# Attention products of two heads, taken in step and in two held bursts

## Chip, core and metric

The kernel runs on one core of a Trainium2 chip. The metric is the device time of one execution in microseconds (us). Three runs of the kernel before gave 765.85, 768.72 and 768.73 us, median 768.72. The profile comes from one more execution.

## What is computed

Three layers follow each other, for 4 batches of 576 tokens and 512 channels (8 heads of 64). All inputs are float32 or wider and the result is float32.

```python
scores = scale * q @ k.T                       # per batch and head, 576 x 576
scores = where(causal, -1e9, scores + cum[:, None] - cum[None, :])   # cum = cumsum(log f)
attn   = exp(scores - max(scores))
attn   = attn / (sum(attn) + 1e-9)
x      = attn @ v                              # heads put side by side: 4 x 576 x 512
h      = relu(x @ w_in); u, v = halves of h
x      = (u * (w_spatial @ layernorm(v) + b)) @ w_out
k      = relu(mix_k(x) @ w_k)
out    = sigmoid(mix_r(x) @ w_r) * (k * k @ w_v)
```

## The kernel before, in words

**Pairs of heads.** The 32 heads of all batches go in 16 pairs. A pair's queries and keys are loaded, scaled, split in two float16 parts and transposed. `score` (L296) makes the scores, queries on partitions, in four steps `u` of up to 512 columns into PSUM tiles `s`; `rowmax` (L304, VectorE) takes the rows' maxima from them. `mrow` (L314) turns the maxima into a row by one matmul into a tile of the pool `psm`, and the row is written through DRAM into the operand `qA`. `scoreT` (L328) makes the scores a second time, keys on partitions, in four steps into tiles `t` (pool `pst`, two buffers), and ScalarE's exponential writes them to `e` (L339), one tile per head, four buffers. `causal` (L341, GpSimd) puts zeros above the diagonal of each of the five key chunks `c` of 128 tokens (the last has 64).

**Products and sums.** `pv` (L365) multiplies the chunks of `e` with the values: the stationary operand is 128x64, head 0 of the pair in columns 0 to 63 and so on partitions 0 to 63 of the output `o`, head 1 in columns 64 to 127. `o` is a tile of two PSUM banks in the pool `pso`, which has one buffer. Chunk 0 gives 512 and 64 columns, chunks 1 to 4 give 448, 320, 192 and 64. `sums` (L346) adds up the rows of `e` by a 128x32 block of ones, with four column blocks: two heads times the query ranges 0 to 383 and 384 to 575. Its output is a tile of `psm`, which holds 2 buffers and serves the MLP matmuls too. `e`, `v` and the ones are float32, and every such matmul stands as two records in the profile, so one pair has 24 records of `pv` and 32 of `sums`.

**After a pair.** ScalarE copies the sums (L358, L360) and the product (`head`, L383); the sums go through DRAM, are inverted, come back spread over the partitions as `sr` (`recip`), and GpSimd multiplies (`norm`, L400) and, with ScalarE, splits the result in the float16 tiles `xt` (`xhi`, `xlo`, L403 and L407).

**MLP and the end.** Of each batch, once its four pairs are there, `m1v`, `m1u` and `m2` (L516, L570, L587) run on TensorE between the attention of later pairs; the last batch's come after the attention. When the attention's pool is given back, its room is taken for the weights of the last layers, which are converted on ScalarE and VectorE; from about 457 us on TensorE works on those layers (L728).

**Order.** `plan_attention` (L623) and `plan_mlp` (L594) give every step a due time and a priority, `run` calls them in that order, and the framework's scheduler then puts the instructions of each engine in an order by priority and by when it takes them to be ready. The engines keep that order. Head `g` has its second scores at time `g`, so the two heads of a pair are one time unit apart; `sums` and `pv` come at `g + 1` and later, of priority 5. The scheduler may put any instruction that is ready between them.

Of the kernel before, what the change touches and what calls it, by code (L numbers as in the profile page):

```python
# [7 lines left out]
F32 = mybir.dt.float32  # L8
# [13 lines left out]
KB = [(128 * c, 128) for c in range(4)] + [(512, 64)]  # L22
# [6 lines left out]


P = dict(load=-8.0, sq=-5.6, ss=-5.2, sc=-5.0, hik=-4.6, lok=-4.25, hiq=-4.2, loq=-3.95, aux=-3.6,
         s=-2.4, m=-0.65, t=0.0, pv=1.0, out=1.35, rc=1.4, nr=1.9, xs=2.2, xl=2.4, mlp=2.7, mlplen=7.0, vload=-5.0, vsq=-3.0,
         w1=-3.8, w0=1.0, wsp=4.6)


def f32(ap):
# [3 lines left out]
class K:  # L40
# [273 lines left out]
    def mrow(self, p):  # L314

        nc = self.nc
        n, m = self.nm16[p % 2], self.nm[p % 2]
        nc.vector.tensor_copy(n[:, 0:10], m)
        nc.vector.tensor_tensor(n[:, 10:20], m, n[:, 0:10], ALU.subtract)
        ps = self.psm.tile([128, 512], F32, tag="m", name="mrow")  # L320
        nc.tensor.matmul(ps[:, 0:128], n, self.ident, start=True, stop=True)
        r = self.at.tile([20, 128], F16, tag="mr", bufs=2, name="mr")
        nc.vector.tensor_copy(r, ps[0:20, 0:128])
        d = self.hl.tile([2, 1280], F16, tag="md", bufs=2, name="md")
        nc.sync.dma_start(d.rearrange("i (c t) -> (i c) t", t=128), r)
        nc.sync.dma_start(self.T["qA", p % 3][67:69].rearrange("p c t -> p (c t)"), d)
# [14 lines left out]
    def causal(self, g, c):  # L341
        n = min(128, KB[c][1])
        e = self.e[g][:, EO[c]:EO[c] + n]
        self.nc.gpsimd.affine_select(out=e, in_=e, pattern=[[1, n]], compare_op=ALU.is_ge, fill=0.0, base=0, channel_multiplier=-1)  # L344

    def sums(self, p):  # L346

        o = self.psm.tile([128, 512], F32, tag="m", name="sums")
        last = {0: 2, 1: 4}
        for x, c in ((0, 0), (1, 0), (1, 1), (0, 1), (1, 2), (1, 3), (0, 2), (1, 4)):  # L350
            q0, q1 = ((0, 384), (384, 576))[x]
            f = max(q0, KB[c][0])
            off = EO[c] + f - KB[c][0]
            for h in range(2):
                r = 64 * h + 32 * x
                self.nc.tensor.matmul(o[r:r + 32, f - q0:q1 - q0], self.ones4 if c == 4 else self.ones[:, 0:32], self.e[2 * p + h][:, off:off + q1 - f], start=(c == 0), stop=(c == last[x]))  # L356
        t = self.at.tile([128, 384], F32, tag="sm", bufs=2, name="sm")
        self.nc.scalar.copy(t[:, 0:192], o[:, 0:192])  # L358
        for r in (slice(0, 32), slice(64, 96)):
            self.nc.scalar.copy(t[r, 192:384], o[r, 192:384])  # L360
        self.rd = [self.hl.tile([2, 576], F32, tag=f"rd{i}", bufs=2, name=f"rd{i}") for i in range(2)]
        self.nc.sync.dma_start(self.rd[0][:, 0:384], t[0:128:64])
        self.nc.sync.dma_start(self.rd[0][:, 384:576], t[32:128:64, 0:192])

    def pv(self, p, hf):  # L365

        b, pr = divmod(p, 4)
        if hf == 0:
            self.o[p] = self.pso.tile([128, 1024], F32, tag="o", name="o")
        o, v = self.o[p], self.v[b % 2]  # L370
        q0, q1 = ((0, 64), (64, 576))[hf]
        cs = [c for c in range(5) if KB[c][0] < q1]
        for c in cs:
            f = max(q0, KB[c][0])
            off = EO[c] + f - KB[c][0]
            for h in range(2):
                r = slice(64 * h, 64 * h + 64)
                self.nc.tensor.matmul(o[r, 448 + f:448 + q1], v[:, c, pr, r], self.e[2 * p + h][:, off:off + q1 - f], start=(c == 0), stop=(c == cs[-1]))  # L378

    def head(self, p):  # L380

# [232 lines left out]
    def add(self, t, prio, fn, *args):  # L614
        self.steps.append((t, prio, len(self.steps), fn, args))
# [7 lines left out]
    def plan_attention(self):  # L623
        add, G = self.add, self.B * self.H
        for p in range(G // 2):
            T = 2.0 * p
            if p > 1:
                add(T + P["load"], 9, self.load, p, "k")
                add(T + P["load"] + 0.3, 9, self.load, p, "q")
            for i, nm in enumerate("kq"):  # L630
                add(T + P["sq"] + 0.1 * i, 2, self.qksq, p, nm)
            add(T + P["ss"], 2, self.qkscale, p)
            add(T + P["hik"], 2, self.qkhi, p, "k", "act")
            add(T - 4.2, 2, self.crow, p)
            add(T + P["lok"], 2, self.qklo, p, "k")
            add(T + P["hiq"], 2, self.qkhi, p, "q", "dve")
            add(T + P["loq"], 2, self.qklo, p, "q")
            add(T + P["aux"], 2, self.kaux, p)
            add(T + P["aux"] + 0.1, 2, self.qaux, p)
            for h in range(2):  # L640
                for u in range(4):
                    add(T + P["s"] + h + 0.22 * u, 4, self.score, 2 * p + h, u)
                    add(T + P["s"] + h + 0.22 * u + 0.05, 1, self.rowmax, 2 * p + h, u)
            add(T + P["m"], 0, self.mrow, p)
        for g in range(G):
            for u in range(4):
                add(g + P["t"] + 0.22 * u, 0, self.scoreT, g, u)
            for c, u in ((0, 0), (1, 1), (2, 2), (3, 2), (4, 3)):
                add(g + P["t"] + 0.22 * u + 0.06, 1, self.causal, g, c)
            if g % 2:  # L650
                add(g + P["pv"], 5, self.sums, g // 2)
                for hf in range(2):
                    add(g + P["pv"] + 0.1 + 0.3 * hf, 5, self.pv, g // 2, hf)
                add(g + P["out"] + 0.1, 1, self.head, g // 2)
                add(g + P["rc"], 1, self.recip, g // 2)
                add(g + P["nr"], 2, self.norm, g // 2)
                add(g + P["xs"], 2, self.xhi, g // 2)
                add(g + P["xl"], 2, self.xlo, g // 2)
        for b in range(self.B):
            for c in range(5):  # L660
                add(8 * b + P["vload"] + 0.2 * c if b else -3.2, 9, self.vload, b, c)
                add(8 * b + P["vsq"] + 0.3 * c, 3, self.vsq, b, c)
            add(8 * b + P["vsq"] + 1.8, 3, self.vscale, b)
# [222 lines left out]
```

## Time and profile before

| | before |
|---|---|
| runs, median of 3 | 768.72 us |
| profiled execution, its own time | 764.88 us |
| its span, first to last instruction | 762.8 us |
| TensorE busy (matmuls) | 693.1 us, 91% |
| VectorE, ScalarE, GpSimd busy | 416.2, 377.1, 158.3 us |
| mean granted TensorE clock | 0.977 |

Busy time is the union of an engine's instructions in the span. In the timeline a matmul lasts until its last value is out, which overlaps the next matmul; in the chain of waits a piece counts only the time that it adds to the chain. PEclk is the granted TensorE clock as a share of 2.4 GHz.

### The profile page before, as it was taken

The page shows a single profiled execution, that of the slowest core. Times are in us where ns is not written, and L with a number is a line of the kernel's source. Part 1 is how long each engine was busy: PE and PEld are TensorE (multiplying, and loading weights), DVE is VectorE, ACT ScalarE, POOL GpSimd, SP SyncE. Part 2 cuts the span into 40 slices and gives each one's busy share as a digit, 9 for nine tenths or more (in the row PEclk, how much of TensorE's full clock was granted, in tenths as well). Part 3 has the DMA queues.
Part 4 walks back from the last instruction along what each step waited for, and adds up shares of the span by engine and source line. Part 5 has one row for each costly group of instructions (what it writes and reads, how often), then busy time and mean ns, then how long its engine had stood idle before and what let it go on. Part 6 is the DMA issues. An engine that isn't in the chain of part 4 may idle for free.

```text
span 762.8 us, 11881 instructions
## 1 busy us (share of the span) xinstructions
PE 693.1 (91%) x4166; PEld 469.0 (61%) x4166; DVE 416.2 (55%) x1147; ACT 377.1 (49%) x772; POOL 158.3 (21%) x369
## 2 busy tenths in 40 slices
PE   0378969999999999999998679999999999999997
PEld 0233433455665556655665448788888888888896
DVE  4886656477545556546014878987415522542342
ACT  4626666676535754346413737757325423622431
POOL 6022523555313533335012200000000000000000
PEclk9998979999999999999999889999999999999999
DMA  9985597476366333320014455460101100010010
GB/s 220 200 195 116 111 181 130 103 158 144 90 168 145 65 70 68 98 54 17 17 50 141 160 160 161 135 188 6 56 1 41 56 1 14 1 56 0 1 56 27
DMA packets 130747, 69.82 MB, mean 92 GB/s; under 512 B 114736, under 2 KB 115408, under 8 KB 130688
## 3 DMA queue, kind: packets, MB, share of 16 engines
q1 hardware_dynamic: 128096, 67.89, 36.9%
q10 hardware_dynamic: 2592, 1.19, 0.6%
q8 instruction: 32, 0.52, 0.3%
q14 instruction: 27, 0.22, 0.1%
HBM read 42.06 MB, written 9.79 MB: 68 GB/s over the span
## 4 chain that ended last, share of the span: by engine, by line
PE 69%; DMA 12%; DVE 7%; SPq 3%; ACT 3%; issue 2%; POOL 2%; DVEq 0%; ACTq 0%; POOLq 0%
PE m L728 38%; PE o L378 6%; PE sums L356 4%; PE s L302 4%; PE t L335 4%; PE m1u L570 4%; PE m L587 4%; PE m1v L516 3%; DMA wst<-in_moe_w_in_dram 2%; DMA wst<-in_moe_w_k_dram 2%; DMA v<-in_v_dram 1%; DMA qA<-qT 1%; DVE junk L311 1%; DMA wb<-in_moe_b_spatial_dram 1%; DMA rd<-r 1%
## 5 line engine op out<-in xcount | busy, mean ns | idle before, releaser
L311 DVE CUSTOM_DVE_ANT_0 junk<-s,mask 128x512 bf16<-128x512 f32 (+4 forms) x160 | 76.1, 476 | 68.4 <-PE s L302 61.9
L728 PE MATMUL m<-xx,moe_w_k 128*128 128x512 f32 (+1 forms) x480 | 106.0, 369 | 0.4 <-ACT x L723 0.4
L728 PE MATMUL m<-moe_w_v,k 128*128 128x512 f32 x432 | 104.2, 390 | 0.0
L339 ACT ACTIVATE e<-t,qa 128x512 f32<-128x512 f32 (+1 forms) x128 | 73.9, 591 | 53.9 <-PE t L335 52.1
L728 PEld LDWEIGHTS m<-xx,moe_w_k 128*128 128x128 f32 x480 | 83.9, 188 | 16.9 <-ACT x L723 0.9
L728 PEld LDWEIGHTS m<-moe_w_v,k 128*128 128x128 f32 x432 | 80.7, 188 | 17.0
L344 POOL TENSOR_SCALAR_AFFINE_SELECT e<-e 128x128 f32<-128x128 f32 (+1 forms) x160 | 54.5, 355 | 155.3 <-ACT e L339 153.4
L378 PE MATMUL o<-e,v 128*64 128x64 f32 (+4 forms) x384 | 76.8, 408 | 1.4 <-POOL e L344 1.3
L302 PE MATMUL s<-kT,qT 128*128 128x512 f16 (+2 forms) x192 | 56.0, 305 | 19.6 <-DVE nm L311 11.8
L764 DVE TENSOR_TENSOR tmp<-tmp 128x512 f32<-128x512 f32 (+1 forms) x40 | 25.5, 638 | 86.7 <-ACT tmp L763 86.7
L728 PE MATMUL m<-gh,moe_w_out 128*128 128x512 f32 (+1 forms) x240 | 55.3, 381 | 3.5 <-DVE u L590 3.4
L763 ACT ACTIVATE tmp<-m 128x512 f32<-128x512 f32 (+1 forms) x40 | 22.1, 556 | 70.2 <-PE m L728 70.2
L570 PE MATMUL m1u<-xt,win 128*128 128x288 f16 x384 | 53.0, 291 | 3.9 <-ACT u L572 3.9
L516 PE MATMUL m1v<-win,xt 128*128 128x512 f16 x240 | 56.5, 379 | 0.0
L302 PE MATMUL s<-kA,qA 67*128 67x512 f16 (+2 forms) x192 | 51.0, 304 | 5.8 <-DMA kA<-kT 3.9
L587 PE MATMUL m<-wspT,vn 128*128 128x288 f16 x384 | 53.9, 291 | 1.3 <-DVE u L590 1.3
L335 PE MATMUL t<-qA,kA 69*128 69x512 f16 (+2 forms) x192 | 51.0, 291 | 1.7 <-ACT e L339 1.7
L728 PEld LDWEIGHTS m<-gh,moe_w_out 128*128 128x128 f32 x240 | 43.3, 193 | 13.3 <-DVE u L590 3.7
L728 PE MATMUL m<-moe_w_r,xx 128*128 128x512 f32 x216 | 51.2, 394 | 0.0
L335 PE MATMUL t<-qT,kT 128*128 128x512 f16 (+2 forms) x192 | 51.1, 290 | 0.0
L570 PEld LDWEIGHTS <-win 128*128 128x128 f16 x384 | 36.6, 99 | 18.5 <-issue 7.8
L728 PEld LDWEIGHTS m<-moe_w_r,xx 128*128 128x128 f32 x216 | 40.4, 187 | 9.9
(164 smaller groups left out, 1061.2 us busy)
## 6 DMA issues: line engine op xcount, KB each, us to landing
sr<-rd SPq DMA_DIRECT2D x32, 144.0 KB
gd<-u SPq DMA_DIRECT2D x16, 288.0 KB
out_dram<-o SPq DMA_DIRECT2D x18, 256.0 KB
knat<-in_k_dram SPq DMA_DIRECT2D x32, 128.0 KB
v<-in_v_dram SPq DMA_DIRECT2D x32, 128.0 KB
g<-gd SPq DMA_DIRECT2D x16, 256.0 KB
wst<-in_moe_w_k_dram SPq DMA_DIRECT2D x8, 512.0 KB
wst<-in_moe_w_v_dram SPq DMA_DIRECT2D x8, 512.0 KB
```

Of the source, the lines that this page charges most:

```text
L302: self.nc.tensor.matmul(s[:, o:o + n], self.tok(qn, p, h, 128 * ib - 64, 128)[0:r], self.tok(kn, p, h, k0, n)[0:r], start=(j == 0), stop=( ...
L311: self.nc.vector.tensor_tensor_reduce(out=self.junk[r0:, 0:n], in0=self.s[u % 2][r0:, o:o + n], in1=self.mask[r0:, m0:m0 + n], op0=ALU.add ...
L335: self.nc.tensor.matmul(t[:, o:o + n], self.tok(kn, p, h, 128 * c, 128)[0:r], self.tok(qn, p, h, q0, n)[0:r], start=(j == 0), stop=(j == 1))
L339: self.nc.scalar.activation(self.e[g][:, 512 * u:512 * u + n], t[:, 0:n], AF.Exp, scale=self.qa[p][:, 5:6])
L344: self.nc.gpsimd.affine_select(out=e, in_=e, pattern=[[1, n]], compare_op=ALU.is_ge, fill=0.0, base=0, channel_multiplier=-1)
L356: self.nc.tensor.matmul(o[r:r + 32, f - q0:q1 - q0], self.ones4 if c == 4 else self.ones[:, 0:32], self.e[2 * p + h][:, off:off + q1 - f], ...
L378: self.nc.tensor.matmul(o[r, 448 + f:448 + q1], v[:, c, pr, r], self.e[2 * p + h][:, off:off + q1 - f], start=(c == 0), stop=(c == cs[-1]))
L516: nc.tensor.matmul(self.m1p, xt[:, xs, 128 * j:128 * j + 128], self.win[:, ws, kc, 512:1024], start=(kc == 0 and n == 0), stop=(kc == 3 an ...
L570: self.nc.tensor.matmul(o, self.win[:, ws, kc, fs], self.xt[(4 * b + kc) % 8][:, xs, ts_], start=(kc == 0 and n == 0), stop=(kc == 3 and n ...
L587: nc.tensor.matmul(o, pairs[n][0], pairs[n][1], start=(n == 0), stop=(n == 13))
L728: self.nc.tensor.matmul(out, l, r, start=(first and j == 0), stop=(last and j == len(pairs) - 1))
L764: nc.vector.tensor_tensor(tmp[:, 0:n], tmp[:, 0:n], tmp[:, 0:n], ALU.mult)
```

## The change

The two heads of a pair go in step: `scoreT` and `causal` of step `u` come for the even head at `0.44 u` and for the odd head 0.22 later, from the same start. `products` replaces the calls of `sums` and `pv`. Part 0 is the product of chunks 0 and 1; part 1 is the sums and then the product of chunks 2, 3 and 4. Within a part every matmul depends on the one before it by `chain` (an order on TensorE, no wait), and all are traced at a priority raised by 300. The sums go into columns 0 to 383 of `o` itself instead of a tile of `psm`; their chunks come in another order; and the tile of `mrow` is one of the score tiles `s` (pool `pss`, two buffers). The arithmetic is the same.

```diff
+         ... t=0.0, tu=0.44, th=0.22, pv0=0.2, pv1=0.9, out=1.35, ...
+PRIO = 300
@@ mrow
-        ps = self.psm.tile([128, 512], F32, tag="m", name="mrow")
+        ps = self.pss.tile([128, 512], F32, tag="s", name="mrow")
@@ new
+    def chain(self, ins):
+        if self.last is not None:
+            self.tc.add_manual_dep(ins.ins, self.last.ins.name, mybir.DependencyInfo(mybir.DependencyClass.NoSync, mybir.DependencyReason.DATA))
+        self.last = ins
+
+    def products(self, p, part):
+        self.last = None
+        with self.tc.high_priority(PRIO):
+            if part == 0:
+                self.o[p] = self.pso.tile([128, 1024], F32, tag="o", name="o")
+                self.pv(p, ((0, 64, 576), (1, 64, 576), (0, 0, 64)))
+            else:
+                self.sums(p)
+                self.pv(p, ((2, 64, 576), (3, 64, 576), (4, 64, 576)))
@@ sums
-        o = self.psm.tile([128, 512], F32, tag="m", name="sums")
-        for x, c in ((0, 0), (1, 0), (1, 1), (0, 1), (1, 2), (1, 3), (0, 2), (1, 4)):
+        o = self.o[p]
+        ends = ((0, 2), (3, 0))
+        for x, c in ((1, 3), (0, 0), (1, 4), (1, 2), (0, 1), (1, 1), (0, 2), (1, 0)):
...
-            for h in range(2):
+            for h in (1, 0):
...
-                self.nc.tensor.matmul(..., start=(c == 0), stop=(c == last[x]))
+                self.chain(self.nc.tensor.matmul(..., start=(c == ends[x][0]), stop=(c == ends[x][1])))
@@ pv
-        q0, q1 = ((0, 64), (64, 576))[hf]
-        cs = [c for c in range(5) if KB[c][0] < q1]
-        for c in cs:
+        for c, q0, q1 in pieces:
...
-            for h in range(2):
+            for h in (1, 0):
@@ plan_attention
+            h = g % 2
-                add(g + P["t"] + 0.22 * u, 0, self.scoreT, g, u)
+                add(g - h + P["t"] + P["tu"] * u + P["th"] * h, 0, self.scoreT, g, u)
...
-                add(g + P["pv"], 5, self.sums, g // 2)
-                for hf in range(2):
-                    add(g + P["pv"] + 0.1 + 0.3 * hf, 5, self.pv, g // 2, hf)
+                add(g + P["pv0"], 5, self.products, g // 2, 0)
+                add(g + P["pv1"], 5, self.products, g // 2, 1)
```

**First place: TensorE, the first pair's products and sums.** Before, `e_403` is head 0 and `e_485` head 1; L378 are products, L356 sums.

```order
L356 MATMUL sums_580<-e_485,ones_121 32x192
L356 MATMUL sums_580<-e_403,ones_121 32x256
L378 MATMUL o_618<-e_485,v0_142 64x512
L378 MATMUL o_618<-e_403,v0_142 64x448
L356 MATMUL sums_580<-e_485,ones_121 32x256
L356 MATMUL sums_580<-e_403,ones_121 32x192
L378 MATMUL o_618<-e_485,v0_142 64x448
L378 MATMUL o_618<-e_403,v0_142 64x320
L356 MATMUL sums_580<-e_485,ones_121 32x192
L356 MATMUL sums_580<-e_403,ones_121 32x192
```

Head 0 is one chunk ahead of head 1 in the products, so that 512 columns of one stand beside 448 of the other, and sums stand between. After the change (`e_423` is head 1, `e_403` head 0; L376 are sums, L394 products):

```order
L376 MATMUL o_516<-e_423,ones_121 32x192
L376 MATMUL o_516<-e_403,ones_121 32x192
L376 MATMUL o_516<-e_423,ones_121 32x128
L376 MATMUL o_516<-e_403,ones_121 32x128
L376 MATMUL o_516<-e_423,ones_121 32x192
L376 MATMUL o_516<-e_403,ones_121 32x192
L394 MATMUL o_516<-e_423,v0_142 64x320
L394 MATMUL o_516<-e_403,v0_142 64x320
L394 MATMUL o_516<-e_423,v0_142 64x192
L394 MATMUL o_516<-e_403,v0_142 64x192
L394 MATMUL o_516<-e_423,v0_142 64x64
L394 MATMUL o_516<-e_403,v0_142 64x64
```

Equal chunks of the two heads stand side by side, and sums and products are apart. Over the whole program the 192 products stand in 89 uninterrupted stretches before and in 39 after, the 256 sums in 44 and in 32: the sums of every pair are in two pieces, of 4 and of 12 matmuls, with other work between.

**Second place: TensorE, the last pair's sums.** The rows `m_` are the MLP's L587 (L603 after the change), 14 matmuls to a number; the third batch has 8 such numbers. Before:

```order
L587 MATMUL m_4398<-wspT,v_105 128x288
L378 MATMUL o<-e,v_143 64x448
L378 MATMUL o<-e,v_143 64x320 x2
L356 MATMUL sums<-e,ones 32x384 x2
L356 MATMUL sums<-e,ones 32x192 x4
L356 MATMUL sums<-e,ones 32x256 x2
L356 MATMUL sums<-e,ones 32x192 x4
L356 MATMUL sums<-e,ones 32x128 x2
L356 MATMUL sums<-e,ones_123 32x64 x2
L587 LDWEIGHTS vn
L587 MATMUL m_4442<-wspT,vn 128x288
```

After:

```order
L603 MATMUL m_4535<-wspT,v_105 128x288
L376 MATMUL o<-e,ones_123 32x64 x2
L376 MATMUL o<-e,ones 32x192 x2
L376 MATMUL o<-e,ones 32x256 x2
L376 MATMUL o<-e,ones 32x192 x2
L376 MATMUL o<-e,ones 32x128 x2
L376 MATMUL o<-e,ones 32x192 x2
L603 LDWEIGHTS v_105
L603 MATMUL m_4535<-wspT,v_105 128x288
L603 LDWEIGHTS vn
L603 MATMUL m_4552<-wspT,vn 128x288
```

`m_4398` is the first of the third batch's eight numbers, `m_4535` the sixth. Behind the last sums stand 210 matmuls of `m2`, 48 of `m1v` and 96 of `m1u` before, and 141, 44 and 96 after: 69 of `m2` and 4 of `m1v` have moved ahead of them.

## Rows read from the trace of the kernel before

**Rows 1.** Windows: busy time of each engine by stage, granted clock, DMA share.

```profile
core 0: us, PE busy (x) PEld busy (x) DVE busy (x) ACT busy (x) POOL busy (x), PEclk, DMA share, GB/s
40.00:117.00 77.00, 62.89 (x372) 28.38 (x371) 49.94 (x193) 44.05 (x99) 23.84 (x50) 0.89 0.75 152
117.00:392.00 275.00, 270.88 (x2056) 153.76 (x2056) 145.53 (x523) 149.83 (x331) 108.11 (x243) 0.99 0.42 90
```

**Rows 2.** Waits of TensorE from 117 to 392 us: total, times, longest.

```profile
PE o L378 <- POOL e L344: 1.3, 1, 1.3
```

**Rows 3.** The same windows, products (L378) alone.

```profile
40.00:117.00 77.00, 14.83 (x74) 5.00 (x74) 0.89 0.75 152
117.00:392.00 275.00, 61.99 (x312) 22.80 (x311) 0.99 0.42 90
```

**Rows 4.** The same windows, sums (L356) alone.

```profile
40.00:117.00 77.00, 13.22 (x96) 4.45 (x96) 0.89 0.75 152
117.00:392.00 275.00, 29.78 (x416) 16.05 (x416) 0.99 0.42 90
```

**Rows 5.** Chain of waits, first pair, broken up (start, us, what).

```profile
59.34 0.76 PE sums L356 x3
61.34 0.77 PE sums L356 x8
65.00 0.68 PE o L378 x3
66.13 0.47 PE o L378 x3
```

**Rows 6.** Chain of waits, one pair from 319 us on.

```profile
319.70 1.00 PE o L378 x3
320.87 0.90 PE o L378 x3
324.03 1.55 PE sums L356 x24
325.74 1.01 PE o L378 x6
327.74 0.26 PE o L378 x2
```

**Rows 7.** Timeline of TensorE: products without a break, and a pair's first 20 ns.

```profile
95.19 2.69 PE L378 MATMUL o<-e,v 128*64 128x512 f32 x16
...
207.28 0.64 PE L378 MATMUL o<-e,v 128*64 128x512 f32 x2
```

**Rows 8.** Chain of waits, around the last pair's sums and behind them.

```profile
335.31 2.59 PE m1v L516 x12
...
387.87 1.55 PE sums L356 x24
389.42 1.83 PE m L587 x14
400.38 1.42 POOL xo L400
457.54 10.21 PE m L728 x36
```

**Rows 9.** Chain of waits, early.

```profile
95.53 2.23 DMA rd<-r
99.67 7.51 DMA wb<-in_moe_b_spatial_dram
```

**Rows 10.** Groups of instructions: busy, mean ns of one, idle before.

```profile
L339 ACT ACTIVATE e<-t,qa 128x512 f32<-128x512 f32 (+1 forms) x128 | 73.9, 591 | 53.9 <-PE t L335 52.1 <-PE s L302 1.2
L344 POOL TENSOR_SCALAR_AFFINE_SELECT e<-e 128x128 f32<-128x128 f32 (+1 forms) x160 | 54.5, 355 | 155.3 <-ACT e L339 153.4 <-DVE nq L270 0.8
L383 ACT COPY xo<-o 128x576 f32<-128x576 f32 x16 | 10.2, 638 | 15.2 <-PE o L378 15.1
L360 ACT COPY sm<-sums 32x192 f32<-32x192 f32 x32 | 9.8, 307 | 0.2
```

More of the change, by code (lines that the diff above doesn't have):

```diff
@@ L31 @@
 P = dict(load=-8.0, sq=-5.6, ss=-5.2, sc=-5.0, hik=-4.6, lok=-4.25, hiq=-4.2, loq=-3.95, aux=-3.6,
-         s=-2.4, m=-0.65, t=0.0, pv=1.0, out=1.35, rc=1.4, nr=1.9, xs=2.2, xl=2.4, mlp=2.7, mlplen=7.0, vload=-5.0, vsq=-3.0,
+         s=-2.4, m=-0.65, t=0.0, tu=0.44, th=0.22, pv0=0.2, pv1=0.9, out=1.35, rc=1.4, nr=1.9, xs=2.2, xl=2.4, mlp=2.7, mlplen=7.0, vload=-5.0, vsq=-3.0,
          w1=-3.8, w0=1.0, wsp=4.6)
+PRIO = 300
 def f32(ap):
@@ L344, in causal @@
         self.nc.gpsimd.affine_select(out=e, in_=e, pattern=[[1, n]], compare_op=ALU.is_ge, fill=0.0, base=0, channel_multiplier=-1)
+    def chain(self, ins):
[11 more added lines that the diff above has]
+                self.pv(p, ((2, 64, 576), (3, 64, 576), (4, 64, 576)))
     def sums(self, p):
-        o = self.psm.tile([128, 512], F32, tag="m", name="sums")
-        last = {0: 2, 1: 4}
-        for x, c in ((0, 0), (1, 0), (1, 1), (0, 1), (1, 2), (1, 3), (0, 2), (1, 4)):
+        o = self.o[p]
+        ends = ((0, 2), (3, 0))
+        for x, c in ((1, 3), (0, 0), (1, 4), (1, 2), (0, 1), (1, 1), (0, 2), (1, 0)):
             q0, q1 = ((0, 384), (384, 576))[x]
@@ L353, in sums @@
             off = EO[c] + f - KB[c][0]
-            for h in range(2):
+            for h in (1, 0):
                 r = 64 * h + 32 * x
-                self.nc.tensor.matmul(o[r:r + 32, f - q0:q1 - q0], self.ones4 if c == 4 else self.ones[:, 0:32], self.e[2 * p + h][:, off:off + q1 - f], start=(c == 0), stop=(c == last[x]))
+                self.chain(self.nc.tensor.matmul(o[r:r + 32, f - q0:q1 - q0], self.ones4 if c == 4 else self.ones[:, 0:32], self.e[2 * p + h][:, off:off + q1 - f], start=(c == ends[x][0]), stop=(c == ends[x][1])))
         t = self.at.tile([128, 384], F32, tag="sm", bufs=2, name="sm")
@@ L363, in sums, with pv @@
         self.nc.sync.dma_start(self.rd[0][:, 384:576], t[32:128:64, 0:192])
-    def pv(self, p, hf):
+    def pv(self, p, pieces):
         b, pr = divmod(p, 4)
-        if hf == 0:
-            self.o[p] = self.pso.tile([128, 1024], F32, tag="o", name="o")
         o, v = self.o[p], self.v[b % 2]
-        q0, q1 = ((0, 64), (64, 576))[hf]
-        cs = [c for c in range(5) if KB[c][0] < q1]
-        for c in cs:
+        for c, q0, q1 in pieces:
             f = max(q0, KB[c][0])
             off = EO[c] + f - KB[c][0]
-            for h in range(2):
+            for h in (1, 0):
                 r = slice(64 * h, 64 * h + 64)
-                self.nc.tensor.matmul(o[r, 448 + f:448 + q1], v[:, c, pr, r], self.e[2 * p + h][:, off:off + q1 - f], start=(c == 0), stop=(c == cs[-1]))
+                self.chain(self.nc.tensor.matmul(o[r, 448 + f:448 + q1], v[:, c, pr, r], self.e[2 * p + h][:, off:off + q1 - f], start=(c == 0), stop=(c == 4 or q1 == 64)))
     def head(self, p):
@@ L645, in plan_attention @@
         for g in range(G):
+            h = g % 2
             for u in range(4):
-                add(g + P["t"] + 0.22 * u, 0, self.scoreT, g, u)
+                add(g - h + P["t"] + P["tu"] * u + P["th"] * h, 0, self.scoreT, g, u)
             for c, u in ((0, 0), (1, 1), (2, 2), (3, 2), (4, 3)):
-                add(g + P["t"] + 0.22 * u + 0.06, 1, self.causal, g, c)
+                add(g - h + P["t"] + P["tu"] * u + P["th"] * h + 0.06, 1, self.causal, g, c)
             if g % 2:
-                add(g + P["pv"], 5, self.sums, g // 2)
-                for hf in range(2):
-                    add(g + P["pv"] + 0.1 + 0.3 * hf, 5, self.pv, g // 2, hf)
+                add(g + P["pv0"], 5, self.products, g // 2, 0)
+                add(g + P["pv1"], 5, self.products, g // 2, 1)
                 add(g + P["out"] + 0.1, 1, self.head, g // 2)
```

## The prediction, before the changed kernel had run

> **What bounds the kernel now.** I read the windows by stage first, then the same windows for the two lines that the change moves, then the waits of TensorE, then single stretches of the chain and the timeline. In the windows [rows 1] the reader sees two stages. From 117 to 392 us TensorE is busy 270.88 of 275 us, VectorE 145.53, ScalarE 149.83, GpSimd 108.11, and the DMA engines 42%: TensorE alone bounds it, and a microsecond less of its work is a microsecond. From 40 to 117 us TensorE is busy 62.89 of 77 us at a granted clock of 0.89 of 2.4 GHz, so a part of that stage ran at 1.2 GHz, and transfers take their turn in the chain. In that first bound stage TensorE hardly waits: the longest wait of a product was one of 1.3 us, for the mask [rows 2].
>
> The products take 61.99 us of the bound stage [rows 3] and the sums 29.78 us [rows 4]. These are 312 of 384 and 416 of 512 records, so 13 of the 16 pairs (24 and 32 records each), at 4.77 and 2.29 us a pair.
>
> Next I looked at what a product costs where. Two matmuls of the two heads run beside each other: a stretch of 16 records takes 2.69 us, and two records, of 512 and 448 columns, had both begun within 20 ns [rows 7]. In such a pair the longer one sets the time. Broken up, a fragment costs 1.00 us when its longer member has 512 columns, 0.90 with 448 [rows 6], 0.68 with 320, 0.47 with 192 [rows 5] and 0.26 with 64 [rows 6]. The order of the kernel before puts head 0 a chunk ahead of head 1. The ladder of one pair is then 64 alone, 64 beside 512, 512 beside 448, 448 beside 320, then 320, 192 and 64 in one stretch, and 64 alone: 0.26 + 1.00 + 1.00 + 0.90 + 1.01 + 0.26 = 4.43 us, near the 4.77 busy, in which the tails overlap other work.
>
> **The change, part by part.** *Products in step.* Equal chunks stand side by side, so each length is paid once. Part 0 is 512, 448 and 64: 1.00 + 0.90 + 0.26 = 2.16. Part 1 is 320, 192 and 64: 0.68 + 0.47 + 0.26 = 1.41. Joined stretches are cheaper: the 16 records of rows 7, whose longer members are 512, 448, 320 and 192, would be 3.05 us in fragments and took 2.69, so each of the three seams costs 0.12. With four seams less the two parts are 1.92 + 1.17 = 3.09 us. The gain is 4.43 - 3.09 = 1.34 a pair, 17 us for 13 pairs. In 7 pairs other work still divides a part, 0.12 each, so I take 16. If no seam were saved it would be 4.43 - 3.57 = 0.86 a pair, 11 us; that is the other end.
>
> The trace speaks for this term, a rule speaks against it. The Trainium skill, page "TensorE: Matmul & The Clock Gate", Part 3, says that a weight load overlaps running matmuls only where their row groups differ; both heads here use all 128 rows and differ in columns only. By that rule the heads would run one after the other, holding them together would win nothing, and the sum would lose its 16 us. The trace disagrees: the two records that began within 20 ns have the same rows [rows 7].
>
> *Sums.* Where they stand in one stretch, all four column blocks run together in 1.55 us [rows 6]. After the change each pair's sums are in two pieces. The first, 192 and 384 columns for both heads, costs what such a group cost before, 0.76 [rows 5]. The second has 64 + 3 x 192 in its longer block: 1.55 less one piece of 192, which is half of the 0.77 for two [rows 5], 1.17. Together 1.93, and with a tail for each, which busy time counts, 2.07 against 2.29 now. The tail is an estimate, 0.07, from the ladder's 4.77 busy against 4.43 over about five stretches. That is 0.2 a pair, 3 us for the 13; between 1 and 5, because early pairs were in many pieces and late ones in one.
>
> *Early pairs.* The three pairs before 117 us take 14.83 + 13.22 = 28 us [rows 3, 4] and would take 3 x 5.0 = 15, so at most 13 us are there. But TensorE is idle 14 of these 77 us, and the chain passes the DMA of the MLP's bias, 7.51 us [rows 9], whose issue stands on SP's queue behind the first pairs' sums and their way through DRAM. I take 4 us, between 0 and 10.
>
> *MLP work moved ahead.* Behind the last pair's sums comes a chain that TensorE doesn't set: copies, DRAM, `norm` at 400.38 and the weights of the last layers, with L728 from 457.54 on [rows 8]. So the end of those sums at 389.42 is what has to come earlier. In the new order 69 matmuls of `m2` and 4 of `m1v` more stand ahead of it, at 1.83 / 14 = 0.13 and 2.59 / 12 = 0.22 us [rows 8]: 9.9 us, taken as 10. Before, they filled the 11 us between the sums and `norm`, where TensorE had nothing else to do, so that moving them saves nothing behind; it gives back over half of the gain.
>
> *New waits.* The held parts wait for both heads' exponentials and masks, 0.59 and 0.36 us each [rows 10]. In the order some ten matmuls of other work usually stand between the last second score that a part needs and the part, and TensorE waits so little now [rows 2] that I take 2 us in all; the ends are 0 and the 30 us of the rival below. `mrow`'s tile takes one of two score buffers for one matmul and one short copy; it gives the MLP's pool both of its buffers back. I count the two as nothing; the work that hides them is the MLP between 117 and 392 us. Without that cover, before 117 us, a score step waits for that copy, some 0.3 us a pair, one us for three pairs, inside the range.
>
> *SP and GpSimd.* No DMA is added or taken away. The masks keep their number; each pair's ten come in a shorter time, on an engine that is busy 108 of 275 us [rows 1].
>
> **The sum**: -16 - 3 - 4 + 10 + 2 = -11 us. The profiled execution's own time is 764.88 us, which gives 754; the median of the three runs is 768.72, 3.8 above it, so for a median I forecast 757 us, 1.5% less. A difference of 0.5%, 3.8 us, is about what a measurement of this kernel tells from none.
>
> **Rivals.** *The gain is absorbed.* TensorE saves 19 us of work between 117 and 392 us, and 10 go for the moved MLP. If the early stage gives nothing and the remaining 9 are lost to waits of 0.6 us a pair, on scores, transfers or copies that TensorE now reaches sooner, the time stays near 768. For it: the chain of the early stage passes transfers [rows 9]. Against it: no other engine is busy over 55% of the bound stage [rows 1]. Chance 0.20.
>
> *The held parts stall.* TensorE keeps its order, and everything behind a part waits with it, the other head's scores too. If at each of the two parts of 16 pairs it waits for one exponential and one mask, 0.95 us [rows 10], 30 us are added: 787 us. It turns the result to slower from a mean wait of 15 / 32 = 0.47 us a part on. For it: both heads' steps come to ScalarE at once now, with two `t` buffers for both. Against it: the one wait of this kind in the bound stage [rows 2]. Chance 0.08.
>
> *The one buffer of `o`.* The sums lie in `o` now, so the next pair's part 0 waits not only for `head` but for the sums' copies: 0.64 + 2 x 0.31 = 1.25 us on ScalarE [rows 10]. With nothing between the pairs that is 20 us, 777 in all; it decides from three quarters of it on. In the order long stretches of scores and MLP stand between, but for one place (fourth and fifth pair) with six matmuls. The Trainium skill, page "PSUM — Partial Sum Buffer", section "PSUM bank collisions raise a hardware error", says why such a wait can't be left out: two engines must not touch one bank and quadrant at once. No row here shows such a collision. Chance 0.04.
>
> *Heads don't run together*, by the rule above: the 16 us of the products stay away, 757 + 16 = 773. Against it stand the ladder's present times. Chance 0.02.
>
> **How the numbers follow.** Forecast 0.66, all of it faster. No change: 0.20. Slower: 0.08 + 0.04 + 0.02 = 0.14. The range goes down to 744: 6 us if the early pairs give 10, 2 without new waits, 2 from the sums' upper end, and 3 if the stage behind the attention gets shorter by a part of the moved MLP. It goes up to 770, which takes in the first rival. What lies outside is the slower cases and a little below, under 2 in 10.
>
> **What the changed profile would show.** Right: products at about 3.3 us busy a pair and sums at 2.1, together 86 instead of 119.8 us; the last pair's sums end about 11 us earlier, near 378 us; L728 begins as much earlier, and the time from there to the end is the same. Wrong: waits of products or sums for `e` of more than 10 us in all; idle time before part 0 that ends with ScalarE's copy of `o`; products still over 4 us a pair; or the sums' end earlier while L728 begins when it did.

## The result and the profile after

The changed kernel took 746.66 us (median of 4 runs, 744.77 to 748.49) against 768.51 us (4 runs of before beside it). The ratio is 0.972, 95% interval 0.969 to 0.976: 2.8% faster, where 1.5% was forecast. The profiled execution took 748.21 us, 16.7 less than that of before, with a span of 746.5.

The windows by stage, all engines (columns as in [rows 1]):

```profile
40.00:117.00 77.00, 60.13 (x408) 29.79 (x409) 57.49 (x217) 48.55 (x111) 28.34 (x59) 0.84 0.75 166
117.00:392.00 275.00, 264.03 (x2143) 155.74 (x2139) 144.86 (x508) 144.57 (x318) 98.93 (x236) 0.99 0.41 92
```

Products (L394) alone, which answer to [rows 3]:

```profile
40.00:117.00 77.00, 14.82 (x84) 5.95 (x84) 0.84 0.75 166
117.00:392.00 275.00, 39.81 (x300) 19.09 (x300) 0.99 0.41 92
```

Sums (L376) alone, which answer to [rows 4]:

```profile
40.00:117.00 77.00, 6.75 (x96) 2.86 (x96) 0.84 0.75 166
117.00:392.00 275.00, 28.81 (x416) 12.60 (x416) 0.99 0.41 92
```

In the later stage a pair's 24 product records took 39.81 x 24 / 300 = 3.18 us busy, where it was 4.77. The sums lost only 1 us there and halved in the early stage. TensorE is less full now: 264 of 275 us.

Waits of TensorE from 117 to 392 us (total, times, longest), the longest totals, which answer to [rows 2]:

```profile
PE o L376 <- POOL e L347: 3.2, 4, 1.3
PE s L305 <- DMA kA<-kT: 1.9, 1, 1.9
PE mrow L324 <- DVE nmh L322: 1.9, 2, 1.3
PE o L394 <- POOL e L347: 1.2, 1, 1.2
```

The held parts do wait for masks now, sums above all, a little at a time.

Chain of waits (start, us, what): a pair's parts, and the last sums to the last layers, which answer to [rows 6, 8]:

```profile
142.10 1.13 PE o L394 x12
152.24 1.88 PE o L394 x12
...
216.11 1.01 PE o L394 x4
217.66 1.02 PE o L394 x8
221.24 0.81 PE o L376 x6
226.40 1.21 PE o L376 x18
...
379.52 1.24 PE o L376 x18
...
391.57 1.41 POOL xo L416
...
466.04 3.98 PE m L744 x16
```

A held part 0 costs 1.88 us, divided in two 2.03; part 1 costs 1.13; the two pieces of sums 0.8 and 1.2. The last sums end at 380.76 us instead of 389.42.

To see where the 16 us arose I cut the span at the last sums' end. Windows of the kernel before, same columns:

```profile
40.00:120.00 80.00, 65.17 (x385) 29.46 (x384) 52.37 (x209) 46.91 (x107) 25.29 (x55) 0.89 0.75 152
120.00:389.40 269.40, 266.00 (x2019) 150.83 (x2019) 142.80 (x507) 146.02 (x319) 106.66 (x239) 0.99 0.43 91
389.40:762.80 373.40, 353.73 (x1732) 283.69 (x1730) 193.22 (x357) 162.84 (x301) 11.55 (x31) 0.98 0.21 67
```

and of the changed kernel:

```profile
40.00:120.00 80.00, 62.62 (x426) 30.71 (x427) 60.46 (x227) 51.55 (x118) 30.89 (x65) 0.85 0.73 162
120.00:380.70 260.70, 250.24 (x2045) 147.69 (x2044) 139.89 (x493) 140.10 (x307) 95.94 (x228) 0.99 0.42 93
380.70:746.50 365.80, 344.25 (x1663) 275.36 (x1661) 191.34 (x353) 161.25 (x301) 11.77 (x31) 0.98 0.20 67
```

Up to the last sums 8.7 us went, behind them another 7.6. Behind them TensorE had 9.5 us less to do and was idle 1.9 more. Ahead of them, from 120 us on, it had 15.8 us less to do, moved MLP included, and its idle time rose from 3.4 to 10.5 us.

### The profile page after: what moved, and what is told of

Read it like the earlier page. It is cut to its first block, busy times and chain, and to the rows that moved or that the text cites. A ratio compares the mean times of both kernels' runs of the same rounds, so it can differ in the third digit from the quotient of the medians.

```text
span 746.5 us, 11863 instructions
## 1 busy us (share of the span) xinstructions
PE 665.8 (89%) x4166; PEld 459.0 (61%) x4166; DVE 418.2 (56%) x1147; ACT 374.4 (50%) x772; POOL 153.4 (21%) x369
## 4 chain that ended last, share of the span: by engine, by line
PE 60%; DMA 11%; DVE 4%; ACT 3%; POOL 3%; SPq 2%; issue 2%; POOLq 0%; ACTq 0%; DVEq 0%
PE m L744 37%; PE m1v L532 4%; PE m L603 4%; PE m1u L586 3%; PE s L305 3%; PE o L394 3%; PE o L376 3%; PE t L338 3%; DMA sr<-rd 3%; DMA rd<-r 2%; DMA wst<-in_moe_w_k_dram 2%; DMA g<-gd 1%; DMA r<-rd 1%; POOL xo L416 1%; DVE junk L314 1%
## 5 line engine op out<-in xcount | busy, mean ns | idle before, releaser
L347 POOL TENSOR_SCALAR_AFFINE_SELECT e<-e 128x128 f32<-128x128 f32 (+1 forms) x160 | 52.5, 343 | 125.4 <-ACT e L342 124.1
L603 PE MATMUL m<-wspT,vn 128*128 128x288 f16 x384 | 58.3, 295 | 4.4 <-ACT vn L567 2.5
L532 PE MATMUL m1v<-win,xt 128*128 128x512 f16 x240 | 58.5, 385 | 1.6 <-ACT xt L419 1.6
L394 PE MATMUL o<-e,v 128*64 128x64 f32 (+4 forms) x384 | 54.6, 415 | 4.0 <-ACT sm L380 2.4
L338 PE MATMUL t<-qT,kT 128*128 128x512 f16 (+2 forms) x192 | 52.6, 291 | 0.0
L603 PEld LDWEIGHTS <-vn 128*128 128x128 f16 x384 | 37.1, 100 | 17.8 <-ACT vn L567 2.8
```

The costliest lines, as they stand in the source:

```text
L338: self.nc.tensor.matmul(t[:, o:o + n], self.tok(kn, p, h, 128 * c, 128)[0:r], self.tok(qn, p, h, q0, n)[0:r], start=(j == 0), stop=(j == 1))
L394: self.chain(self.nc.tensor.matmul(o[r, 448 + f:448 + q1], v[:, c, pr, r], self.e[2 * p + h][:, off:off + q1 - f], start=(c == 0), stop=(c ...
L532: nc.tensor.matmul(self.m1p, xt[:, xs, 128 * j:128 * j + 128], self.win[:, ws, kc, 512:1024], start=(kc == 0 and n == 0), stop=(kc == 3 an ...
L603: nc.tensor.matmul(o, pairs[n][0], pairs[n][1], start=(n == 0), stop=(n == 13))
```

## Experiments

Every ratio is to the kernel before, run beside it on the same chip.

**1. The tile of `mrow` back in `psm`** (changed kernel otherwise).

```diff
-        ps = self.pss.tile([128, 512], F32, tag="s", name="mrow")
+        ps = self.psm.tile([128, 512], F32, tag="m", name="mrow")
```

> The changed kernel with the row-maxima product back in the MLP's pool. In its order 212 m2 and 42 m1v matmuls stand behind the last sums, as before the change, and not 141 and 44; products and sums stand in 42 and 32 stretches, as in the change (39 and 32). Theory M (the moved MLP work costs its own time and the stage behind the attention gains nothing): the last sums end 9 us earlier than in the changed kernel, near 372, the stage behind keeps its length, the total is 9 us less, near 738. Theory B (work behind the attention counts as much as work ahead of it): the sums end as early, the stage behind is 8 us longer again, the total stays within 3 us of 746.7.

Measured: 752.97 us, ratio 0.980 (0.976 to 0.984). In the order 212 matmuls of `m2` and 42 of `m1v` stand behind the last sums, about as many as before the change. The windows of this kernel, cut at its last sums:

```profile
120.00:378.50 258.50, 246.14 (x1998) 142.15 (x1999) 138.21 (x479) 137.81 (x304) 96.65 (x228) 0.99 0.43 90
378.50:747.60 369.10, 351.69 (x1732) 282.05 (x1730) 193.48 (x358) 162.29 (x301) 10.78 (x31) 0.99 0.21 68
```

The bank of `mrow` is what moves some 70 matmuls of `m2` ahead. Without that move the last sums end only 2.2 us earlier: from 120 us on TensorE has only 4.1 us less to do, though some 9 us of `m2` are gone, because more scores come after 120 us, and it is idle 12.4 us there and not 10.5. What is behind the sums takes 3.3 us longer. So the move is no loss, where the prediction entered one of 10 us. Neither theory had the time: M said 738, B within 3 us of 746.7. Of the 6 us between the medians these windows show 1.1, for this profiled execution was the shortest of its six runs (749.55 us), with a granted clock of 0.99 behind the sums where the changed kernel had 0.98.

**2. `mrow` and the sums in `psm`**: in step and held, but the banks of before. To the edit of experiment 1 comes:

```diff
-        o = self.o[p]
+        o = self.psm.tile([128, 512], F32, tag="m", name="sums")
```

> The changed kernel with the sums too in a tile of the MLP's pool: both changes of banks undone, held bursts and heads in step kept. 210 m2 and 36 m1v behind the last sums, sums in 24 stretches, products in 45. Theory M: as without the banks' change for the row maxima, about 738, or some us more if the MLP's matmuls wait for the pool. Theory B: within 3 us of 746.7. If the new banks are themselves what brings the gain, it goes back to 755 or more.

Measured: 757.34 us, 0.984 (0.980 to 0.988). The time is where it was put if the new banks bring the gain, 755 or more; but over half of the gain remains with neither bank changed, so they bring a part of it.

**3. No raised priority.**

```diff
-PRIO = 300
+PRIO = 0
```

> The changed kernel without the raised priority: 46 stretches of sums and 44 of products instead of 32 and 39, 168 m2 and 47 m1v behind the last sums. If the holding by priority carries the gain: 19 more stretches at 0.12 us and unequal pairs, 3 to 8 us slower, 750 to 755. If heads in step are enough: within 2 us of 746.7.

Measured: 758.35 us, 0.985 (0.981 to 0.990), slower than the 750 to 755 expected if the holding carries the gain. The products stand in 44 stretches and the sums in 46, instead of 39 and 32, and over the whole program the products are busy 60.0 us instead of 54.6, the sums 40.3 instead of 35.6. The changed kernel without `chain`, built but not run, has the same order of instructions on every engine: in this program it is the priority that holds the parts, and the chain adds nothing.

**4. The old ladder inside the held parts.** Head 0 goes one chunk ahead of head 1 within each part.

```diff
-        for c, q0, q1 in pieces:
+        o1 = [(c, q0, q1, 0) for c, q0, q1 in pieces]
+        o2 = [(c, q0, q1, 1) for c, q0, q1 in pieces]
+        both = [o1[0]] + [y for a_, b_ in zip(o2, o1[1:]) for y in (a_, b_)] + [o2[-1]]
+        for c, q0, q1, h in both:
...
-            for h in (1, 0):
+            if True:
```

> The changed kernel with head 0 one chunk ahead of head 1 within each part, in nearly as few stretches (49 of products, 32 of sums). Theory A (the predicted one: two matmuls side by side take the time of the longer, so equal lengths must stand together): part 0 goes from 1.92 to 2.8 us and part 1 from 1.17 to 1.7, 1.4 us a pair, 13 bound pairs, 19 us slower, near 765. Theory Q (each head's column block works off its own matmuls as long as nothing of the whole array stands between; only broken stretches cost): 10 more stretches, 1 to 2 us, near 748.

Measured: 754.62 us, 0.981 (0.977 to 0.986), between theory Q (748) and theory A (765); the trace tells more. Its chain of waits, products alone (the line is L397 here), part 1 and part 0 of one pair and a broken part 0 of the next:

```profile
278.09 1.13 PE o L397 x12
...
282.39 1.88 PE o L397 x12
...
302.24 1.00 PE o L397 x2
303.70 1.87 PE o L397 x8
```

A ladder without a break costs what equal chunks cost: 1.88 and 1.13 us. Each head's block of columns works through its own matmuls; both heads have the same sum of columns in a part, and which chunk stands beside which is of no account. (Blocks of unequal sums were not tried.) What costs is a break behind the first 512 columns: that head then runs alone for 1.00 us, and the other's whole part, 1.87, comes after. So Q has the mechanism, and its price of a break was too low. Part 0 is broken in most pairs, and its products are busy 66.5 us over the program.

**5. The changed kernel again**, beside these.

> The changed kernel once more, beside the next three and the kernel before. Expected 746.7 within 3 us; its profile tells whether the early stage (first m1v at 122 us, before 136) and the stage behind the last sums (365.8 us long, before 373.4) repeat.

Measured: 745.77 us, 0.974 (0.971 to 0.977). The result repeats.

**6. The kernel before with less MLP behind the last sums.**

```diff
-        for n in range(7 * part, 7 * part + 7):
+        for n in ((0, 13)[part],) if b == 2 and 2 * fc + hf > 0 else range(7 * part, 7 * part + 7):
```

> The kernel before with 2 of 14 matmuls left in seven of the third batch's eight m2 numbers, all of which stand behind the last sums: 84 matmuls, 10.2 us of TensorE, less there and none less ahead. (The third batch's spatial product is left out in these places.) Theory M, the predicted step (work behind the last sums fills a time in which TensorE has nothing else to do): the time stays within 2 us of the kernel before. Theory B (this work is on the way to the last layers): 5 to 10 us less.

It leaves out 84 matmuls of the third batch's `m2`. Measured: 756.26 us, 0.987 (0.984 to 0.990), theory B's range. The last sums end where they did, and what is behind them:

```profile
389.10:754.30 365.20, 343.80 (x1648) 274.90 (x1646) 193.16 (x357) 161.83 (x301) 11.22 (x31) 0.98 0.21 68
```

TensorE has 9.9 us less to do there, and the stretch is 8.2 us shorter than the 373.40 of before. The first matmul of the last layers came at 449.11 instead of 457.54 us. So the work behind the last sums is on the path, nearly in full.

**7. The changed kernel with less MLP ahead of the last sums.**

```diff
-        for n in range(7 * part, 7 * part + 7):
+        for n in ((0, 13)[part],) if b == 2 and 2 * fc + hf < 5 else range(7 * part, 7 * part + 7):
```

> The changed kernel with 2 of 14 matmuls left in the first five m2 numbers of the third batch, those that the new order puts ahead of the last sums (60 matmuls, 7.3 us left out; the order then pulls others ahead, so that 31 m2 fewer and 7 m1v more stand ahead, and 29 m2 fewer behind). Theory M: the last sums end 2.3 us earlier and the total falls by 2. Theory B: the total falls by 4 to 7.

It leaves out 60 of the third batch's `m2`. Measured: 747.05 us, 0.974 (0.970 to 0.978): no gain from 60 matmuls less, and neither theory's. Waits of TensorE from 375 to 470 us:

```profile
PE m L603 <- DVE v L573: 6.7, 1, 6.7
PE m1v L532 <- ACT xt L419: 5.7, 1, 5.7
```

and the stretch behind the last sums:

```profile
378.30:746.90 368.60, 344.28 (x1625) 274.76 (x1625) 189.68 (x350) 162.69 (x301) 11.24 (x31) 0.96 0.20 65
```

The sums end 2.4 us earlier, but the scheduler spread the remaining work so that TensorE reaches the last batch's `m1v` earlier and waits 5.7 us (1.6 in the changed kernel) for the last pair's `xt`. The wait for `v` above is 5.7 us in the changed kernel too. Thirty-eight matmuls fewer take the same 344 us, at a granted clock of 0.96 against 0.98. A part of the lower clock stands right at this wait: the wait ends at 390.31 us, and the clock is at 1.2 GHz from 388.5 to 395.3 us, where the changed kernel has 2.4 GHz until 417.8. The changed kernel has come near the point where the last pair's way through DRAM needs what is left to cover it; how much of the missing gain is that wait and how much the clock stays open.

**8. The sums in one stretch.** The product of chunk 4 comes ahead of the sums, so that nothing keeps their two pieces apart.

```diff
+                self.pv(p, ((4, 64, 576),))
                 self.sums(p)
-                self.pv(p, ((2, 64, 576), (3, 64, 576), (4, 64, 576)))
+                self.pv(p, ((2, 64, 576), (3, 64, 576)))
```

> The changed kernel with the product of chunk 4 ahead of the sums, which then wait for the same last piece of e and stand in one stretch (16 instead of 32; the products in 59 instead of 39). One stretch of sums costs 1.55 us, the two pieces 0.78 and 1.21; chunk 4 before it costs 0.26 less a seam and the rest of part 1 some 1.0 instead of 1.13. Theory H (broken stretches cost): 0.3 us a pair, 4 us less, near 743. If TensorE instead waits longer for the last mask: no gain, or some us more.

Measured: 750.96 us, 0.980 (0.977 to 0.983). One piece does cost less, 1.54 us where two cost 0.78 + 1.21, from its chain and its group of products (L395 here):

```profile
276.69 1.54 PE o L377 x24
```

```profile
L395 PE MATMUL o<-e,v 128*64 128x64 f32 (+4 forms) x384 | 57.7, 412 | 10.0 <-POOL e L347 7.4 <-ACT sm L381 2.1 <-ACT e L342 0.6
```

The sums are busy 28.2 us over the program instead of 35.6. But chunk 4's product stands in front of the part and waits 7.4 us for the last mask, and is itself in fragments. TensorE's busy time fell by 2 us (665.8 to 663.8), and the time rose by some 5. Of those 5 the profiled executions show one (749.89 against 748.21 and 748.95 us), so that the rest of the rise isn't explained.

**9. The kernel before with `mrow` in a score tile**, the reverse of the edit of experiment 1.

> The kernel before with one line of the change: the tile of mrow is one of the score tiles s instead of a tile of psm. Theory R (the bank of mrow acts by itself: with mrow out of psm the MLP's products and mrow no longer wait for each other's buffers, so the first m1v comes some 10 us earlier and the work between the attention's steps finds its place): the first m1v near 124 us instead of 135.7, the last pair's sums end 3 to 6 us earlier than 389.4, time 759 to 764 us against 766 to 769 for the kernel before. Theory H (the bank of mrow is worth something only beside held products): the first m1v at 132 to 136 us, time within 2 us of the kernel before.

Measured: 781.54 us, 1.018 (1.014 to 1.021): both theories fell. The group of sums in this kernel:

```profile
L356 PE MATMUL sums<-e,ones 128*32 128x192 f32 (+4 forms) x512 | 52.7, 346 | 5.6 <-POOL e L344 5.6
```

With nothing held, the sums fall into 68 stretches instead of 44, presumably since the new bank changes what the scheduler takes to be ready: 52.7 us instead of 43.0, with 10.8 us idle from 120 us to the last sums instead of 3.4. The same line that gains some 5 us beside held parts (0.980 in experiment 1, 0.974 with it) costs 13 without them.

**10. The heads out of step, the rest of the change kept.**

```diff
-                add(g - h + P["t"] + P["tu"] * u + P["th"] * h, 0, self.scoreT, g, u)
+                add(g + P["t"] + 0.22 * u, 0, self.scoreT, g, u)
...
-pv0=0.2
+pv0=0.3
```

> The changed kernel with the two heads of a pair one time unit apart again, as before the change (scoreT and causal of the odd head come later; part 0 of the products at 0.3 instead of 0.2 so that it follows). Held parts, banks and priority stay. Theory S (going in step is needed: a held part otherwise waits for the later head's exponentials and masks, and TensorE with it): more than 15 us of idle time between 120 us and the last sums (10 in the changed kernel), time 752 to 762 us. Theory N (the step of the heads is worth nothing; the held parts and the banks do all of it): time 744 to 750 us, idle there 8 to 12 us, sums in fewer pieces so that they take some 4 us less of TensorE.

Measured: 756.38 us, 0.984 (0.980 to 0.987). Both of theory S's numbers come out, the time and the idle time. TensorE, from 120 us to the last sums:

```profile
120.00:387.30 267.30, 248.25 (x2001) 145.15 (x1998) 136.99 (x484) 138.15 (x301) 94.46 (x229) 0.97 0.41 90
```

19.1 us idle instead of 10.5. Of these 8.6 us some 4 are waits of the held parts (8.5 against 4.6), and 4.4 are second scores that wait for an exponential (5.2 against 0.8). The group of its products shows what they wait for, and that they are longer, 439 ns in the mean against 415 (403 in experiment 5, so such means vary between executions):

```profile
L394 PE MATMUL o<-e,v 128*64 128x64 f32 (+4 forms) x384 | 59.8, 439 | 10.0 <-POOL e L347 5.0 <-ACT e L342 3.2 <-ACT mv L552 1.7
```

**11. The same with both old banks**: held parts, out of step (the edits of experiments 1, 2 and 10). Equal chunks still stand side by side, sums and products apart.

> As the run before, and both the sums and mrow in tiles of psm again: the held parts alone, without the step of the heads and without the new banks. If holding brings its share by itself, as with both tiles in psm and the heads in step (757.3 us there): 755 to 760 us. Under theory S 763 to 770 us, no faster than the kernel before.

Measured: 750.71 us, 0.978 (0.973 to 0.982). Better than either theory: the parts as they are held here bring 2.2% without the step and without the banks. What those add, to 0.974 (0.971 to 0.977), is not clear of noise. With the old banks, going in step brings no gain over this (experiment 2, 0.980 to 0.988, an interval that meets this one); with the new banks it brings 1% (experiment 10 against 5). The parts of this change don't add. In the profiled executions of experiments 2 and 11 the last sums end at 381.4 and 381.0 us, as early as in the changed kernel, while 210 and 208 matmuls of `m2` stay behind them and the stretch there takes 373.8 and 371.7 us, about as before: the held parts shorten what is ahead of the last sums, and the moved MLP what is behind.

## Why the prediction was right, and where not

The direction, the mechanism of the largest term and the range held. The gain was 16.7 us in the profiled execution instead of 11; the term that was furthest off is that of the moved MLP. The median lies 10 us under the forecast: 5.7 us are the larger gain, and for the rest I had added the 3.8 us between before's profiled execution and its median, while after the change the profiled execution lies 1.6 us above the median.

*Products.* Near in size: forecast 3.09 us a pair in 1.92 + 1.17, measured 1.88 + 1.13, and 4.77 - 3.18 = 1.59 a pair, 21 us for 13 pairs against 16; the forecast had started from a ladder of 4.43 us where 4.77 were busy. The reason given, "Equal chunks stand side by side, so each length is paid once", was wrong: experiment 4 pays the same for unbroken ladders. What the change takes away is breaks. The seam of 0.12 us between aligned pieces was about right (2.03 divided, 1.88 whole: 0.15); a seam in a ladder costs up to 1.00, and the old order had both ladders and breaks. The two heads do run beside each other, and the rule of the Trainium skill, page "TensorE: Matmul & The Clock Gate", Part 3, that a weight load overlaps only with other row groups, does not describe this kernel: a part of twelve records takes 1.88 us, while one head's 512 columns alone take 1.00 (experiment 4). In the trace of the kernel before, around 207.28 us [rows 7], two further weight loads stand from 207.34 to 207.48 us while both heads' matmuls run until 207.88 and 207.93, all of them on 128 rows. The rule speaks of weight loads; that whole heads would then run one after the other was the prediction's own step.

*Sums.* 1 us in the later stage instead of 3. The two pieces cost 0.78 + 1.21 = 1.99, near the 1.93 foreseen, but of the eleven pairs behind the fifth six had the sums in one piece before, of 1.55 [rows 6], and five in two; the saving lay in the early pairs (13.22 to 6.75 us), as the lower end had it. The two pieces are a cost of the change that experiment 8 could not win back.

*Early pairs.* "I take 4 us, between 0 and 10": it was 10, the upper end. In the timeline of the kernel before, the fourth pair's last sums and the end of the fifth's:

```profile
124.13 0.83 PE L356 MATMUL sums<-e,ones 128*32 128x384 f32 x4
126.07 0.84 PE L356 MATMUL sums<-e,ones 128*32 128x192 f32 x8
127.84 0.62 PE L356 MATMUL sums<-e,ones 128*32 128x256 f32 x4
129.82 0.52 PE L356 MATMUL sums<-e,ones 128*32 128x192 f32 x4
130.95 0.51 PE L356 MATMUL sums<-e,ones 128*32 128x192 f32 x8
132.67 0.30 PE L356 MATMUL sums<-e,ones 128*32 128x64 f32 x2
...
147.40 0.30 PE L356 MATMUL sums<-e,ones 128*32 128x64 f32 x2
```

and the same in the changed kernel:

```profile
118.53 0.85 PE L376 MATMUL o<-e,ones 128*32 128x192 f32 x8
120.36 1.28 PE L376 MATMUL o<-e,ones 128*32 128x64 f32 x24
...
135.06 2.35 PE L376 MATMUL o<-e,ones 128*32 128x64 f32 x24
```

Of the fourth pair's sums six pieces are shown, 3.6 us spread over 9; now all of them take 2.1 us in two pieces. The fifth pair's end at 137.41 us instead of 147.70. By these ends both kernels had done the same scores, sums and first MLP matmuls (the changed one 11 product records less), and TensorE had been busy 84.8 us instead of 100.6 and idle 52.6 instead of 47.1. Broken products and sums lasted past the 117 us at which I had ended the early stage. This gain goes with the parts as such: the fifth pair's sums end between 133.9 and 139.5 us in experiments 1, 2, 3, 10 and 11 too, with old banks and new, out of step, and without the raised priority, but at 148.2 us in experiment 9, which has only the bank. From there to the last sums the changed kernel takes 1.6 us more: the moved MLP's 10 and the new idle time eat what the later pairs save.

*MLP work moved ahead.* This is the step that failed: "they filled the 11 us between the sums and `norm`, where TensorE had nothing else to do, so that moving them saves nothing behind". I took the wait for the last pair as what sets the stretch behind the sums. The windows show it differently: TensorE is busy 353.73 of its 373.40 us, and the last two batches' MLP and the last layers all queue on it. Behind the sums 7.6 us went in the changed kernel, and experiment 6 shows the path by itself, 8.2 us for 9.9 us of work. The first matmul of the last layers comes 16 us earlier, 441.5 instead of 457.54, and not 11. So the move costs about nothing in all. How far it carries is limited: experiment 7 met the wait for `xt`.

*New waits.* "2 us in all": 7 us more idle time from 120 us to the last sums. The stated mechanism is there (masks, 4.4 us in the waits above), but no wait is over 2 us and the rest are scores, `mrow` and transfers that TensorE reaches sooner. The term had ends of 0 and 30. Over the whole program sums and products waited 8.9 us for masks (7.7 and 1.2), close to the 10 us that the prediction had named as a sign of being wrong.

*Rivals.* Absorption did not happen. Of the stall of the held parts a little appears out of step (experiment 10): they wait 8.5 us from 120 us to the last sums, in 19.1 us of idle time, and the kernel is still faster than before. The one buffer of `o` cost little: over the whole program the products waited 2.4 us for the sums' copy (L380) and 0.4 for `head` (L399), in the group of products of the changed kernel, shown with its group of sums:

```profile
L394 PE MATMUL o<-e,v 128*64 128x64 f32 (+4 forms) x384 | 54.6, 415 | 4.0 <-ACT sm L380 2.4 <-POOL e L347 1.2 <-ACT xo L399 0.4
L376 PE MATMUL o<-e,ones 128*32 128x192 f32 (+4 forms) x512 | 35.6, 349 | 7.7 <-POOL e L347 7.7
```

Summed up by measured terms: about -10 up to the fifth pair, +1.6 from there to the last sums, -7.6 behind them, -16 in the span.

What stays open: why the held parts, the step and the banks interact as they do. Experiments 1 and 9 show that one line moves the time by some -5 or +13 us depending on the others, through the order that the scheduler finds; which of its choices does it was not traced.

## What to carry to other kernels

In this kernel matmuls that use different columns of the array run beside each other as long as nothing else comes between: hold them together, and don't mind which piece stands beside which. Bringing the data of both to the same time is worth a trial; here it paid 1% with the new banks and nothing clear with the old. Before calling moved work free, count the engine's busy time over the whole stretch behind it, not the wait that comes first there. In a program whose order a scheduler finds, parts of a change don't add, so try them together and apart.

## What the runs showed that I had not expected

Two column blocks are not tied to each other matmul by matmul: an unbroken ladder of 12 records, in which one head is a chunk of 512 columns ahead, takes 1.88 us, as the aligned order does, while one break behind a 512-column matmul costs 1.00 us. In experiment 7 thirty-eight matmuls fewer behind the sums left TensorE's busy time there at 344 us, with a mean granted clock of 0.96 instead of 0.98: in this execution work taken away came back as slower work. It is the longest of four runs, 748.66 us; the others, at a clock of 0.967 to 0.971 over the whole span, took 744.60 to 747.45, so how much of it is usual is not shown.
